# Side B's weights behind batch 2's keys, first products in pairs of blocks, and small work moved between VectorE and GpSimd

## The chip, the cores and the metric

The kernel runs on one core of a Trainium2 chip, as one program. The metric is device time in microseconds (us) of one execution; the kernel before has a median of 203.14 us over 3 runs (202.81 to 203.45). Engines are named as the profile names them: PE is TensorE's matrix products (PEld its weight loads), DVE is VectorE, ACT is ScalarE, POOL is GpSimd, and SP is SyncE, which here only issues transfers.

## The reference

Linear attention for 8 batches, then a mixture of experts with one expert per row:

```
q_s = softmax of q over the head's 64 channels
k_s = softmax of k over the 576 positions
x   = (q_s @ (k_s^T @ v)) for 8 batches x 8 heads x 576 x 64, as 4608 rows of 512
logits = x @ w_gate + modality_bias[modality_id];  e = argmax(logits)
out[row] = softmax(logits)[e] * (relu(x[row] @ w1[e]) @ w2[e])      w1: 512 x 1024, w2: 1024 x 512
```

The bias decides the expert in this draw: rows of modality 0 take one expert, those of modality 1 another. The kernel works with these two, and recomputes at the end if a row should want a third (here no row does).

## The kernel before, in words

**Places.** Each of the 4608 rows gets a place: rows of side A (one modality) fill places from the front, those of side B from the back. The running offsets (`pos`, `aoff`) are worked out on DVE in the first 12 us. From them come `slot` (which row lies in which place, L643 to L648), its digits and one-hot tables (`hhi`, `hv`, `hlo`), which PE turns into the list of rows `idx` (L718), and `bsel` (the bias of each place, L667 to L672).

**Attention, one batch at a time.** q, k and v of a batch (1152 KB each) come by SP's queue into a ring of five buffers `st` (L393). ACT takes the exponent of q in place (L821), DVE sums it (L827), and q is scaled into `eq` (L843): by DVE in batches 0 and 1, by POOL from batch 2 on. ACT takes the exponent of k into `ek` (L854); v is cast into `vb` (L864) by ACT or POOL. PE forms k^T v in two halves (L957), DVE makes `kvbd` of it (L984 to L993). PE transposes and sorts q in groups of 128 positions (L1033), ACT or DVE brings the result out of PSUM as `et` (L1045, L1047), PE multiplies by `kvbd` (L1072), and ACT or DVE copies the result into the places in `xs` (18 copies of a batch, L1103). A buffer of `st` is free for a later load once its last reader is done: the scaling for q, the exponent for k, the cast for v.

**Experts, in 9 passes of 256 places on each side.** A pass needs the batches whose rows fill its places. It has gates (L1138, L1152 to L1166), a first product of 8 blocks of 128 hidden channels, each of 4 matmuls into one PSUM bank (L1202), the relu of each block out of its bank into `hT` (L1172 on ACT, L1174 on DVE), a second product of 8 matmuls for each of two row tiles (L1215), a scaling by the gate into `y_sb` (L1178, L1180), and an indirect store by POOL (L1183). One more tile, where the two sides meet, is done near the end (L1340 to L1364).

**Weights.** `W` holds both sides' experts in bf16, cast on the way by POOL's transfers: four parts of a side (two of w1, two of w2), 8 + 4 transfers (L510, L521). Side A's first waits until k of batch 1 has landed, and q of batch 2 waits until side A's third part has landed (L403). Side B's parts have no such waits; the first two follow side A's, the others come behind `hv`.

**The order.** Each step is an `Op` with a rank and assumed costs on its engine. `Plan.order` plays the program through with these costs (which engine is idle, which ring has a free buffer) and emits the instructions in the order of that play. Each engine then takes its instructions strictly in this order, so a change of one cost or one wait can move instructions on all engines. Dead matmuls (`unread`, L1451) are put into early gaps of PE.

## Time and profile before

| | us |
|---|---|
| median of 3 runs | 203.14 |
| the profiled execution's own time | 204.96 |
| its span, first to last instruction | 203.2 |
| PE busy | 180.4 (89%) |
| DVE busy | 154.5 (76%) |
| ACT busy | 127.9 (63%) |
| POOL busy | 90.5 (45%) |

The page cuts the span into 40 slices of 5.08 us and gives the busy share of each in tenths. PE is at 9 in most slices from 30 us on; DMA is at 9 in most slices up to about 96 us, and low afterwards; loads from memory end near 117 us. The granted clock of TensorE is at half speed in one stretch near 30 us and in a shorter one near 121 us.

### The profile page before, as it was taken

The numbers are of one execution on the slowest core, as the hardware profiler recorded it, in microseconds if no ns is written. First come the engines' busy times: TensorE is split into PE (matmuls) and PEld (weight loads), VectorE is DVE, ScalarE is ACT, GpSimd is POOL, SyncE is SP. The second block draws the span as 40 slices with busy tenths as digits, with TensorE's granted clock in tenths as the row PEclk, the third lists the DMA queues.
The fourth block names the chain that finished last, engine by engine and source line by source line (L and its number), as shares of the span: only waits on it lengthen the run. The fifth ranks groups of instructions, "written<-read, shape, count | busy, mean of one in ns | idle before, by whom it ended". The sixth has DMA issues, their size and how long they took to land.

```text
span 203.2 us, 5008 instructions
## 1 busy us (share of the span) xinstructions
PE 180.4 (89%) x1716; PEld 124.4 (61%) x1735; DVE 154.5 (76%) x447; ACT 127.9 (63%) x283; POOL 90.5 (45%) x113
## 2 busy tenths in 40 slices
PE   0789679989999999999959959999999999999990
PEld 0446348577657486868647735878667657766760
DVE  1899997999879999669968973959589557755660
ACT  2669875998759599999849674999896000000100
POOL 6001910584944489943395086591303311222231
PEclk9999955999999999999999988999999999999998
DMA  6999999999999997999369711111112112121102
GB/s 191 371 400 392 186 203 225 295 394 313 280 411 404 404 399 250 390 404 338 115 201 385 271 52 55 52 53 56 53 55 103 52 55 103 52 103 56 76 28 108
DMA packets 18588, 42.33 MB, mean 208 GB/s; under 512 B 1913, under 2 KB 1913, under 8 KB 18562
## 3 DMA queue, kind: packets, MB, share of 16 engines
q1 hardware_dynamic: 13344, 28.33, 38.4%
q0 software_dynamic: 5200, 13.64, 23.3%
q8 instruction: 14, 0.23, 0.5%
q10 hardware_dynamic: 18, 0.04, 0.2%
q14 instruction: 12, 0.10, 0.1%
HBM read 36.75 MB, written 9.70 MB: 229 GB/s over the span
## 4 chain that ended last, share of the span: by engine, by line
PE 69%; DVE 11%; ACT 6%; issue 5%; POOL 3%; DMA 2%; ACTq 2%; DVEq 0%; POOLq 0%
PE ps L1215 28%; PE ps L1202 26%; DVE xs L1103 3%; PE ps L1033 3%; PE ps L1072 3%; PE ps L957 3%; ACT xs L1103 3%; PE ps L1138 2%; DVE own L827 2%; DMA bias<-n_moe_modality_bias_dram 2%; DVE eq L843 2%; POOL out_dram L1183 1%; ACT vb L864 1%; POOL eq L843 1%; ACTq L1007 1%
## 5 line engine op out<-in xcount | busy, mean ns | idle before, releaser
L1202 PE MATMUL ps<-xs,W 128*128 128x256 bf16 x576 | 71.9, 277 | 0.2
L1215 PE MATMUL ps<-W,hT 128*128 128x512 bf16 (+1 forms) x277 | 66.4, 378 | 1.1 <-issue 0.2
L1183 POOL DMA_INDIRECT out_dram<-y_sb,idx x36 | 35.7, 992 | 57.5 <-DVE y_sb L1180 30.7
L1202 PEld LDWEIGHTS <-W 128*128 128x128 bf16 x576 | 55.2, 99 | 9.8 <-issue 0.9
L1172 ACT ACTIVATE hT<-ps 128x256 bf16<-128x256 f32 x63 | 23.0, 414 | 40.7 <-PE ps L1202 40.4
L1215 PEld LDWEIGHTS <-hT 128*128 128x128 bf16 x296 | 28.6, 99 | 29.3 <-issue 1.3
L1174 DVE TENSOR_SCALAR hT<-ps 128x256 bf16<-128x256 f32 (+1 forms) x83 | 34.6, 427 | 7.4 <-PE ps L1202 4.7
L1180 DVE TENSOR_SCALAR y_sb<-ps,gate 128x512 f32<-128x512 f32 (+1 forms) x28 | 20.1, 720 | 21.1 <-PE ps L1215 15.9
L1103 ACT CAST xs<-ps 128x256 f32 (+1 forms) x99 | 31.8, 447 | 2.1 <-PE ps L957 1.0
L843 POOL TENSOR_TENSOR eq<-st,qi 128x512 bf16<-128x512 f32 (+1 forms) x30 | 28.5, 972 | 6.1 <-PE ps L1202 2.7
L827 DVE TENSOR_REDUCE own<-st 128x18 f32<-128x1152 f32 x16 | 21.6, 1350 | 0.1
L821 ACT ACTIVATE st<-st 128x1152 f32<-128x1152 f32 x16 | 18.7, 1195 | 2.8 <-DMA st<-in_q_dram 2.3
L854 ACT ACTIVATE ek<-st 128x1152 bf16<-128x1152 f32 x16 | 19.1, 1200 | 1.2 <-DMA st<-in_k_dram 1.2
L1045 ACT CAST et<-ps 128x512 bf16<-128x512 f32 (+1 forms) x30 | 16.1, 565 | 5.9 <-PE ps L1033 5.6
L1033 PE MATMUL ps<-perm,eq 128*128 128x128 bf16 x144 | 14.3, 230 | 3.5 <-POOL eq L843 2.0
L1103 DVE CAST xs<-ps 128x256 f32 (+1 forms) x45 | 16.1, 415 | 0.5 <-ACT xs L1103 0.4
L864 POOL CAST vb<-st 128x1152 bf16<-128x1152 f32 x8 | 9.0, 1142 | 16.0 <-DMA st<-in_v_dram 10.0
L1033 PEld LDWEIGHTS <-eq 128*128 128x128 bf16 x144 | 10.0, 101 | 8.2 <-POOL eq L843 3.1
L957 PE MATMUL ps<-vb,ek 64*128 64x129 bf16 x288 | 11.4, 222 | 2.7 <-ACT vb L864 2.5
L957 PEld LDWEIGHTS <-ek 64*128 64x128 bf16 x288 | 8.7, 96 | 6.7 <-issue 2.9
L1072 PE MATMUL ps<-et,kvbd 128*128 128x128 bf16 (+1 forms) x160 | 11.8, 219 | 0.2
L510 POOL DMA_DIRECT2D W<-in_moe_w_dram x8 | 5.1, 674 | 15.2 <-DMA st<-in_k_dram 15.2
(134 smaller groups left out, 170.9 us busy)
## 6 DMA issues: line engine op xcount, KB each, us to landing
st<-in_q_dram SPq DMA_DIRECT2D x6, 1152.0 KB, 12.3
st<-in_k_dram SPq DMA_DIRECT2D x6, 1152.0 KB, 13.7
st<-in_v_dram SPq DMA_DIRECT2D x6, 1152.0 KB, 12.9
st<-in_q_dram SPq DMA_DIRECT2D x4, 576.0 KB, 5.1
st<-in_k_dram SPq DMA_DIRECT2D x4, 576.0 KB, 6.7
st<-in_v_dram SPq DMA_DIRECT2D x4, 576.0 KB, 9.7
W<-in_moe_w_dram POOLq DMA_DIRECT2D x8, 256.0 KB, 6.8
W<-in_moe_w_dram POOLq DMA_DIRECT2D x4, 512.0 KB, 10.4
```

The costliest lines, as they stand in the source:

```text
L827: nc.vector.tensor_reduce(out=sums[qib.idx][:, h * NJ : (h + n) * NJ], in_=view(st[bq.idx], [[Dh, n * NJ], [1, Dh]], h * NJ * Dh), op=ALU.add,
L843: (nc.vector if e == "DVE" else nc.gpsimd).tensor_tensor(out=view(eq[eqb.idx], [[HG * Dh, n], [Dh, HG], [1, Dh]], j0 * HG * Dh), in0=view( ...
L854: nc.scalar.activation(out=view(ek[ekb.idx], [[Dh, n], [HG * Dh, NJ], [1, Dh]], h * Dh), in_=view(st[bk.idx], [[NJ * Dh, n], [Dh, NJ], [1, ...
L957: nc.tensor.matmul(out=ps_t[kvp[hg].idx][:, 130 * hp : 130 * hp + 129], lhsT=ek[ekb.idx][rows, j, P * hp : P * hp + P], rhs=vb[vbb.idx][ro ...
L1033: nc.tensor.matmul(out=view(t, [[2 * nj * 64, 2], [1, 64]], hp * nj * 64 + jj * 64), lhsT=eq[eqb.idx][:, j0 + jj, P * hp : P * hp + P], rh ...
L1103: w_ = nc.scalar.copy(out=dst, in_=src) if e == "ACT" else nc.vector.tensor_copy(out=dst, in_=src)
L1172: nc.scalar.activation(out=dst, in_=src, func=ACT.Relu)
L1174: nc.vector.tensor_scalar_max(out=dst, in0=src, scalar1=0.0)
L1180: nc.vector.tensor_scalar(out=dst, in0=src, scalar1=g, scalar2=None, op0=ALU.mult)
L1183: s_ = nc.gpsimd.indirect_dma_start(out=out, out_offset=bass.IndirectOffsetOnAxis(ap=ix[:, c : c + 1], axis=0), in_=ysb, in_offset=None, b ...
L1202: m = nc.tensor.matmul(out=t[:, 0:w], lhsT=w1(W[:, slot_, :], kd, f), rhs=xs[:, kd, lo : lo + w], start=(kd == 0), stop=(kd == KD - 1),)
L1215: nc.tensor.matmul(out=t, lhsT=h[:, kf, i * P : (i + 1) * P], rhs=W[:, slot_, W2 + kf * D + c0 : W2 + kf * D + c0 + cn], start=(kf == 0), ...
```

## The change

Side B's first part of `W` waits for k of batch 2 (POOL waits there), and q of batch 3 waits for side B's third part (SP waits there). All of batch 2's loads are planned ahead of side B's weights. `slot` and `bsel` go from DVE to POOL, and batch 2's q is scaled by DVE. The first product puts two blocks of 256 columns in one bank, and one relu takes both out. The loading of the modality ids and of the bias become two steps. Some assumed costs change, and the last passes' drains of POOL's queue.

```diff
 def dma(nbytes):
-    busy = nbytes / 390e3
+    busy = nbytes / 383e3
...
-            if src is q and b == 2:
-                behind(d, issued["w", 0, 2][-1], "the weights come first")
+            if src is q and b in (2, 3):
+                behind(d, issued["w", b - 2, 2][-1], "the weights come first")
...
-    l_ids = pl.op({"ACT": (1.2, 3.5)}, load_ids, rank=-9)
+    l_ids = pl.op({"ACT": (0.6, 3.6)}, load_ids, rank=-9)
+    l_bias = pl.op({"ACT": (0.6, 3.9)}, load_bias, rank=-8)
...
-            if not s and not part:
-                behind(issued["w", 0, 0][0], issued[k.tensor.name, 1], "the first batches come first")
+            if not part:
+                behind(issued["w", s, 0][0], issued[k.tensor.name, s + 1], "the batches ahead come first")
...
     def slot_run(_):
-        d = nc.vector
+        d = nc.gpsimd
...
     def bsel_run(_):
-        d = nc.vector
+        d = nc.gpsimd
...
-    w_in = [[load_w(0, part) for part in range(4)], []]
-    for part, nms in enumerate(("q", "k", "v", "")):
-        for nm in nms:
-            load_one(nm, 2)
-        w_in[1].append(load_w(1, part))
-    for o in w_issue[1][2:]:
-        pl.later(o, o_hv[-1])
+    w_in = [[load_w(0, part) for part in range(4)]]
+    load_batch(2)
+    w_in.append([load_w(1, part) for part in range(4)])
+    for before, o in zip([loads["k", 2][0][-1]] + w_issue[1], w_issue[1]):
+        pl.later(o, before)
...
-            if b <= 1:
+            if b <= 2:
                 ncost = on_dve(n_, 1, True)
...
+        for i in range(2):
+            for kd in range(KD):
+                f = f0 + i
+                m = nc.tensor.matmul(
+                    out=t[:, i * w : (i + 1) * w],
...
-        for f in range(KF):
+        for f in range(0, KF, 2):
...
-                    lambda e, f=f, fb=fb: relu(e, hT[hb.idx][:, f, 0:w], ps_t[fb.idx][:, 0:w]),
+                    lambda e, f=f, fb=fb: relu(
+                        e, hT[hb.idx][:, f : f + 2, 0:w], view(ps_t[fb.idx], [[w, 2], [1, w]])
+                    ),
```

What this does to the order is shown at three places. Lines of the kernel after are 1 to 9 higher than those of before.

On POOL, in the first 45 us: before, the two experts' numbers are read (`eid_i`) as soon as the constants are made, and `hv` stands between side B's first two and last two parts of `W` (64 partitions: w1; 128 partitions: w2).

```order
L353 MEMSET ex_99 128x2
L539 TENSOR_LOAD eid_i
...
L510 DMA W<-in_moe_w_dram 64x2x1024
L701 TENSOR_TENSOR hv<-hhi,vals 128x432 x6
L521 ISA
L521 DMA W<-in_moe_w_dram 128x2x1024
...
L1183 DMA out_dram<-y_sb_83,idx 4608x512
L843 TENSOR_TENSOR eq_70<-st_65,qi_86 128x512 x3
```

Now `slot` and `bsel` stand ahead of the read, and `hv` ahead of all of side B:

```order
L645 TENSOR_TENSOR slot<-na,kt 128x72
...
L670 TENSOR_TENSOR bsel<-isb,biasd 128x288
L673 TENSOR_TENSOR bsel<-bsel,bias_b 128x288
L674 TENSOR_SCALAR krow<-isb,keyd,key 128x36
L541 TENSOR_LOAD eid_i
...
L523 DMA W<-in_moe_w_dram 128x2x1024
L703 TENSOR_TENSOR hv<-hhi,vals 128x432 x6
L512 ISA
L512 DMA W<-in_moe_w_dram 64x2x1024
...
L1183 DMA out_dram<-y_sb_82,idx 4608x512
```

All four parts of side B stand behind one wait for k of batch 2, and the stores of the first pass behind them; batch 2's scaling is gone from here.

On ACT, in side A's first pass (about 31 to 36 us): before, four relus of one block each stand ahead of the first copy of batch 1 into `xs` (the copies need batch 1's last product).

```order
L1172 ACTIVATE hT_80<-ps_91 128x256
L1172 ACTIVATE hT_80<-ps_92 128x256
L1172 ACTIVATE hT_80<-ps_91 128x256
L1172 ACTIVATE hT_80<-ps_92 128x256
L1157 ACTIVATE ex_98<-L,gmx 128x8 x2
L1157 ACTIVATE ex_99<-L,gmx 128x8 x2
L1103 REGISTER_ALU
L1103 ISA
L1103 COPY xs<-ps_94 128x4x64
```

Now three relus of two blocks each stand there:

```order
L1172 ACTIVATE hT_80<-ps_92 128x2x256
L1172 ACTIVATE hT_80<-ps_91 128x2x256
L1157 ACTIVATE ex_98<-L,gmx 128x8 x2
L1172 ACTIVATE hT_80<-ps_92 128x2x256
L1157 ACTIVATE ex_99<-L,gmx 128x8 x2
L1103 REGISTER_ALU
L1103 ISA
L1103 COPY xs<-ps_94 128x4x64
```

Six blocks of the first product instead of four are ahead of batch 1's last product on PE, and so ahead of these copies.

On ACT, near the arrival of the last load, v of batch 7 (about 111 to 120 us): before, ACT casts one half of it, and relus stand behind the cast.

```order
L821 ACTIVATE st_65<-st_65 128x1152 x2
L1178 ACTIVATE y_sb_85<-ps_91,gate 128x512
L854 ACTIVATE ek_69<-st_64 128x2x9x64
L864 CAST vb_73<-st_63 128x2x9x64
L1172 ACTIVATE hT_80<-ps_95 128x256
L1172 ACTIVATE hT_80<-ps_91 128x256
L1172 ACTIVATE hT_80<-ps_93 128x256
```

Now ACT has no cast there:

```order
L821 ACTIVATE st_65<-st_65 128x1152
L1178 ACTIVATE y_sb_85<-ps_90,gate 128x512
L821 ACTIVATE st_65<-st_65 128x1152
L1172 ACTIVATE hT_80<-ps_96 128x2x256
L1172 ACTIVATE hT_80<-ps_91 128x2x256
L854 ACTIVATE ek_69<-st_67 128x2x9x64
```

POOL casts both halves instead, with batch 6's scaling behind them:

```order
L843 TENSOR_TENSOR eq_71<-st_63,qi_87 128x256
L1183 DMA out_dram<-y_sb_84,idx 4608x512
L864 CAST vb_73<-st_63 128x2x9x64
L1183 DMA out_dram<-y_sb_85,idx 4608x512
L864 CAST vb_73<-st_63 128x2x9x64
L843 TENSOR_TENSOR eq_70<-st_66,qi_86 128x512 x4
```

What waited for the last load on two engines waits for it on one.

## Rows read from the trace of the kernel before

**Rows 1.** The page's slices: PE busy, granted clock, DMA busy, in tenths.
```profile
PE   0789679989999999999959959999999999999990
PEclk9999955999999999999999988999999999999998
DMA  6999999999999997999369711111112112121102
```

**Rows 2.** Waits of PE: start, us, what [idle before <- releaser].
```profile
30.48 3.57 PE L1202 MATMUL ps<-xs,W 128*128 128x256 bf16 x16
41.85 0.35 PE L1138 MATMUL ps<-wg_sb,xs 128*128 128x8 bf16 x8 [0.85 <-ACT xs L1103]
44.45 1.33 PE L718 MATMUL ps<-hv,xs 128*128 128x72 bf16 x36
54.41 0.69 PE L957 MATMUL ps<-vb,ek 64*128 64x129 bf16 x18
57.42 3.62 PE L1215 MATMUL ps<-W,hT 128*128 128x512 bf16 x15
104.21 0.40 PE L1033 MATMUL ps<-perm,eq 128*128 128x128 bf16 x4 [2.03 <-POOL eq L843]
118.90 0.61 PE L1138 MATMUL ps<-wg_sb,xs 128*128 128x8 bf16 x16 [2.03 <-ACT hT L1172]
```

**Rows 3.** Stretches: length, busy time (instructions) of each engine, PEclk, DMA share, GB/s.
```profile
10.00:20.00 10.00, 9.22 (x97) 5.31 (x96) 9.88 (x33) 8.08 (x10) 0.60 (x1) 1.00 1.05 397
20.00:25.00 5.00, 3.10 (x44) 1.80 (x42) 4.78 (x14) 4.59 (x8) 5.00 (x9) 0.96 1.09 200
30.40:34.80 4.40, 4.40 (x34) 3.40 (x31) 3.36 (x17) 2.12 (x8) 0.00 (x0) 0.50 1.12 217
120.40:123.20 2.80, 2.77 (x8) 0.84 (x9) 0.87 (x1) 1.11 (x2) 2.53 (x3) 0.50 0.24 92
```

**Rows 4.** SP's issues of loads, and the landing times of L393's transfers.
```profile
30.84 0.37 SPq L393 DMA_DIRECT2D st<-in_q_dram  x1
109.07 0.37 SPq L393 DMA_DIRECT2D st<-in_v_dram  x1
DMA to landing us min/median/max: 4.2/10.7/23.3
```

**Rows 5.** POOL in order of time.
```profile
19.40 2.65 POOL L510 DMA_DIRECT2D W<-in_moe_w_dram  x4 [15.16 <-DMA st<-in_k_dram]
65.02 2.24 POOL L864 CAST vb<-st 128x1152 bf16<-128x1152 f32 x2 [1.94 <-DMA st<-in_v_dram]
99.69 2.23 POOL L864 CAST vb<-st 128x1152 bf16<-128x1152 f32 x2 [6.02 <-PE ps L957]
105.38 3.67 POOL L843 TENSOR_TENSOR eq<-st,qi 128x512 bf16<-128x512 f32 x4
118.84 0.98 POOL L1183 DMA_INDIRECT out_dram<-y_sb,idx  x1 [0.16 <-ACT hT L1172]
```

**Rows 6.** ACT in order of time.
```profile
42.39 1.30 ACT L821 ACTIVATE st<-st 128x1152 f32<-128x1152 f32 x1
117.41 1.16 ACT L864 CAST vb<-st 128x1152 bf16<-128x1152 f32 x1 [2.45 <-DMA st<-in_v_dram]
```

**Rows 7.** Groups by form: line, engine, operation, count | busy us, mean ns | idle before.
```profile
L843 POOL TENSOR_TENSOR eq<-st,qi 128x512 bf16<-128x512 f32 x24 | 24.9, 1060 | 6.1 <-PE ps L1202 2.7 <-DVE qi L839 2.4 <-ACT ex L1157 0.7
L1174 DVE TENSOR_SCALAR hT<-ps 128x256 bf16<-128x256 f32 x81 | 33.2, 421 | 6.7 <-PE ps L1202 4.7 <-PE ps L1138 0.6 <-ACT hT L1172 0.2
L1172 ACT ACTIVATE hT<-ps 128x256 bf16<-128x256 f32 x63 | 23.0, 414 | 40.7 <-PE ps L1202 40.4
L1045 ACT CAST et<-ps 128x512 bf16<-128x512 f32 x24 | 14.2, 604 | 5.2 <-PE ps L1033 4.9
L843 DVE TENSOR_TENSOR eq<-st,qi 128x512 bf16<-128x512 f32 x8 | 5.2, 684 | 0.0
L1174 DVE TENSOR_SCALAR hT<-ps 128x512 bf16<-128x512 f32 x2 | 1.4, 692 | 0.7 <-PE ps L1351 0.5
```

More of the change, by code (lines that the diff above doesn't have):

```diff
@@ L435, in load_ids, with load_bias @@
         )
+    def load_bias(_):
         nc.scalar.dma_start(
@@ L495, in experts @@
         d.tensor_sub(out=keyd, in0=key[:, 1:2], in1=key[:, 0:1])
-    o_parts = pl.op({"DVE": (0.35, 0.5)}, parts_run, [l_ids, c_dve], rank=-5)
+    o_parts = pl.op({"DVE": (0.35, 0.5)}, parts_run, [l_bias, c_dve], rank=-5)
     o_spread = pl.op({"PE": (0.2, 0.45)}, spread_run, [o_parts, c_pool], rank=-5, takes=[b_buf])
@@ L756 @@
     o_off = pl.op({"DVE": (1.0, 1.2)}, off_run, [o_pos], rank=-5, uses=[r_buf])
-    o_vals = pl.op({"DVE": (0.7, 0.85, True)}, vals_run, [c_dve2], rank=15)
-    o_slot = pl.op({"DVE": (1.17, 1.3, True)}, slot_run, [o_off], rank=15)
-    o_digits = pl.op({"DVE": (0.5, 0.65, True)}, digits_run, [o_slot], rank=15)
+    o_vals = pl.op({"DVE": (0.7, 0.85)}, vals_run, [c_dve2], rank=-4)
+    o_slot = pl.op({"POOL": (1.3, 1.45, True)}, slot_run, [o_off], rank=12)
+    o_digits = pl.op({"DVE": (0.5, 0.65, True)}, digits_run, [o_slot], rank=12)
     o_hhi = [pl.op(on_dve(HC * NSL // 3), hhi_run(i), [o_digits], rank=15) for i in range(3)]
@@ L767 @@
     o_idx = pl.op({"DVE": (0.4, 0.6)}, idx_run, [o_id], rank=16, uses=[id_buf])
[L768 removed]
+    o_bsel = pl.op({"POOL": (1.8, 2.0, True)}, bsel_run, [o_off, o_exp], rank=13)
     o_mid = pl.op({"DVE": (1.0, 1.15, True)}, mid_run, [o_idx, o_bsel], rank=74)
[L771 to L777 removed]
+    w_in = [[load_w(0, part) for part in range(4)]]
[3 more added lines that the diff above has]
+        pl.later(o, before)
     for b in range(3, B):
@@ L1198, in w1, with h_mm @@
         return view(t, [[2, P]], kd * F + f // 2 * 2 * P + f % 2)
-    def h_mm(t, lo, w, slot_, f, whole=False):
-        for kd in range(KD):
-            m = nc.tensor.matmul(
-                out=t[:, 0:w],
-                lhsT=w1(W[:, slot_, :], kd, f),
-                rhs=xs[:, kd, lo : lo + w],
-                start=(kd == 0),
-                stop=(kd == KD - 1),
-            )
-            if whole and not f and not kd:
-                for w_ in final[-2:]:
-                    sync(m, w_, "every batch is in its places")
+    def h_mm(t, lo, w, slot_, f0, whole=False):
+        for i in range(2):
[3 more added lines that the diff above has]
+                    out=t[:, i * w : (i + 1) * w],
+                    lhsT=w1(W[:, slot_, :], kd, f),
+                    rhs=xs[:, kd, lo : lo + w],
+                    start=(kd == 0),
+                    stop=(kd == KD - 1),
+                )
+                if whole and not f and not kd:
+                    for w_ in final[-2:]:
+                        sync(m, w_, "every batch is in its places")
     def y_mm(t, h, i, slot_, c0=0, cn=D):
@@ L1243, in ffn @@
         )
-        g3 = pl.op({"DVE": (0.18, 0.36)}, lambda _: gates3(t0, nt, ex[xb.idx]), [g2], rank=rank_g, uses=[xb])
+        g3 = pl.op({"DVE": (0.32, 0.45)}, lambda _: gates3(t0, nt, ex[xb.idx]), [g2], rank=rank_g, uses=[xb])
         hs = []
-        for f in range(KF):
+        for f in range(0, KF, 2):
             fb = Buf(r_ps)
             hm = pl.op(
-                on_pe(*[w] * KD),
+                on_pe(*[w] * (2 * KD)),
                 lambda _, f=f, fb=fb: h_mm(ps_t[fb.idx], lo, w, side, f, whole),
@@ L1302, in ffn @@
         if n >= 5 and not last:
-            pl.op({"POOL": (3.0, 3.0)}, lambda _: nc.gpsimd.drain(), [st_], rank=-1)
+            drain = lambda _: nc.gpsimd.drain()
+            if (n, lo, w) == passes_a[-1]:
+                pl.op({"POOL": (2.0, 2.0)}, drain, evs, rank=-0.5)
+            else:
+                pl.op({"POOL": (3.0, 3.0)}, drain, [st_], rank=-1)
         return g3
@@ L1424, in ffn_rest @@
         ym = pl.op(
-            on_pe(*[D] * KF), y_rest(fb), [*hs, *wc], rank=500 + rank + 0.2, takes=[fb], uses=[hb, wb[1]]
+            on_pe(*[D] * KF), y_rest(fb), [*hs, *wc], rank=500 + rank + 0.4, takes=[fb], uses=[hb, wb[1]]
         )
```

5 lines of the change are left out of this document (2 added, 3 removed).

## The prediction

> **What bounds the kernel now.** I read the page's slices first: PE is busy in nearly all of them from the seventh on, and DMA in nearly all up to the nineteenth [rows 1]. So two things run side by side until about 96 us, and after 124 us PE runs alone. With PE full over most of the span, a change helps only where it takes away PE's idle time, its half-clock time, or the start-up ahead of the first expert product at 30.48 us [rows 2]. I therefore went through PE's waits in order of time, and for each to the engine named and that engine's own wait.
>
> Between 30.5 us and 124 us there are four places of size. (a) The granted clock is 0.50 from 30.4 to 34.8 [rows 3]: 4.4 us at 1.2 instead of 2.4 GHz, 2.2 us lost. (b) At 41.85 PE has waited 0.85 us for ACT's copies of batch 1 into `xs` [rows 2]. (c) At 104.21 it has waited 2.03 us for POOL's scaling of batch 5 [rows 2], which stands on POOL behind the casts of batch 6's v at 99.69 [rows 5]; I read that start as the landing of that v, since the PE work named there had long been done. (d) At 118.90 it has waited 2.03 us for ACT's relus [rows 2], because ACT stood 2.45 us for the last load, v of batch 7, before its cast at 117.41 [rows 6]; then the clock is 0.50 from 120.4 to 123.2 [rows 3], another 1.4 us. The rest are waits of half a microsecond and less, mostly behind DVE's copies of batch 2 into `xs`, 1.5 us together by my estimate.
>
> **The change part by part.** *The weights' waits.* q of batch 2 is issued at 30.84 as before, since it waits for the same third part of side A [rows 4]. Now nothing of side B travels with it. 1.18 MB at 397 GB/s [rows 3] are 3.0 us. The shortest landing is 4.2 us [rows 4], of a transfer of half that size, which leaves 2.7 us of set-up. So q2 lands at 36.5, k2 at 39.5, v2 at 42.4. POOL began side A's weights at 19.40 [rows 5] and the third part had landed at 30.84: 11.4 us for three parts, and 2.6 us for each further one (0.52 MB written at 200 GB/s [rows 3]). Side B's parts then land at about 45.7, 48.3, 50.9 and 53.5, and q of batch 3 at 56.6. PE comes to side B's first product only after side A's second pass and batch 2's sorting, at about 54, so some 5 us cover the new wait. Behind the waiting POOL stand only side B's own transfers and the first stores (`hv` is ahead of it); behind the waiting SP the rest of batch 3. Both set-ups lie beside a transfer in flight (v2, then side B's fourth part), so I cost them at 0; uncovered they are 2.7 us each. The gain is at most one part, 2.6 us; I take the stream of loads as 1 us earlier, since batch 3's v lands near 62.5 and was cast at 65.02 as it landed [rows 5], and part of that is given back to the stores.
>
> The Trainium skill, "DMA: Bandwidth & Descriptors" (Rules for kernel authors), says to issue a transfer early and wait late, so that the fixed set-up overlaps; this change issues two groups later. That bears on the mechanism of the first rival.
>
> *`slot` and `bsel` on POOL, batch 2's scaling on DVE.* Eight forms of small instructions go ahead of side A's weights on POOL. The nearest row is the 512-element scaling at 1060 ns [rows 7]; as an upper end that is 8.5 us from 12 us on, so 20.5 against the 19.40 at which POOL stops waiting for k of batch 1; a lower end is 2 us. I take 3, hidden by that wait: 0, and at most 1.1 us later weights. DVE gives these up and takes four scalings of 684 ns and a half one, 3.1 us: even. POOL is freed of 4.9 us near 50 us, where it was not the bound.
>
> *Blocks in pairs.* A pair costs DVE 692 ns instead of 2 x 421, ACT about 604 (a 512-column copy, the nearest row) instead of 2 x 414 [rows 7]. With 40 and 32 pairs that is 6.0 us of DVE and 7.2 us of ACT. Neither is the bound, so I credit only 0.6 us, out of the 1.5 us of small waits.
>
> *What the order makes of it.* On PE six blocks of A's first product instead of four come ahead of batch 1's last product. At 3.57 us for 16 matmuls [rows 2], at the low clock, the 8 more delay it by 1.8 us, and with it ACT's copies and, behind them, the exponent of q2 (42.39 before [rows 6]), to 44.2 or later. So the earlier landing of batch 2 is not used. Wait (b) would grow to 2.7, but the 1.33 us of `idx` products [rows 2] now stand ahead of it: net +0.5 to +1.4, I take 0.9. Then k^T v of batch 2, which ran at 54.41 [rows 2], is wanted at about 50, while ACT has its operands only at about 51: +1.0. By the second product of B's first pass (57.42 before [rows 2]) PE is 2 us behind on the same work.
>
> *The last loads.* v7 is issued at 109.07, when POOL has ended the scaling of batch 5 (105.38 + 3.67) [rows 4, 5], and that chain starts with v6's landing at 99.7. With the stream 1 us earlier, batch 5's scaling begins 1 us earlier and one store fewer stands ahead of it (0.98 [rows 5]), just when PE comes: wait (c) goes, -2.0. v7 lands at 116.4. ACT no longer stands at its cast, so (d) in its old form goes: -2.0 and -1.4. PE alone is then at +0.9 +1.0 -0.6 -2.0 -2.0 -1.4 = -4.1 us.
>
> What is late next is POOL: two casts (2.23), one store (0.98) and the first scaling of batch 6 (1.06) [rows 5, 7] end 4.3 us after v7, at 120.7. Before, PE passed that point at 123.8 (gates and a block from 118.90, eight second products that end at 123.2, batch 7's first k^T v of 0.7 [rows 2, 3]). So the end moves by -3.1, not by -4.1: PE waits 1.0 there, too little to expect a fall of the clock, as after (c). The other scalings of batch 6 follow at 1.06 us each between PE's other work: +0.4.
>
> Sum: -4.1 + 1.0 + 0.4 = -2.7 us. (a) and the start-up stay as they are: the scaling of batch 1 on DVE, which paces PE up to 30 us, is not touched, and the steps before it change places at equal length. The profiled execution took 204.96 us for its span of 203.2; so 202.3 by its count, and against the median of 203.14, 200.4 us.
>
> **Rivals.** *First, slower: the two waits open the loads' queue.* If a set-up of 2.7 us lies bare at k2 and again before q3, the stream is up to 5.4 us late where it is full, and v7 with it. From v7 on all is fixed: the scaling of batch 6 is there at v7 + 4.3, and 0.4 is lost behind it. So the change is slower once v7 lands after 119.1, 1.7 us later than before. With v7 3.1 us late: 203.14 + 1.4 = 204.5. For it: DMA's slices have been full with no wait there [rows 1]. Against it: other transfers are in flight at both moments.
>
> *Second: the stream gains more.* If the freed time of POOL, DVE and ACT lets buffers come free 3 us earlier, v7 lands before 115, POOL's chain ends before PE needs it, and what is left is PE alone, -4.1, with some of the +1.9 at the start hidden: 198.4. For it: 13 us of relu time saved. Against it: relus are not what frees a buffer.
>
> *Third: the clock.* The new fillers around batch 1's k^T v could keep TensorE at 2.4 GHz through A's first product: -2.2, and the 1.8 us of delay halves. Alone this ends at POOL's chain and changes nothing; with the second rival it gives 196.5. The opposite, a fall after the longer wait at 42 us, costs 1.4 and is hidden in the same way unless v7 is early.
>
> *Fourth: no difference.* The +1.9 at the start stays, and (c) and (d) only change their names, within 0.6 us of 203.14.
>
> **How the numbers follow.** The forecast 200.4, with its own range 199.2 to 202.4, gets 0.40; the second and third rival 0.25; no difference 0.14; the first rival and others on its side 0.21. Less than 0.3% (0.6 us) can't be told from no change here. So faster 0.40 + 0.25 = 0.65, same 0.14, slower 0.21. The range goes from 197.2, between the two better cases, to 204.5, the first rival's time.
>
> **What would show it.** Right: ACT has no wait for v near 117, PE's last long wait names POOL's `eq`, the wait near 42 us for ACT's copies is above 1.3 us, and v7 lands between 115 and 117. The step on the weights is wrong if PE's first product of side B waits for a transfer, or if DMA shows an empty stretch between 30 and 60 us. The step on the start is wrong if the granted clock is 1.00 at 32 us, or if A's first product begins more than 1 us away from 30.5. The whole is wrong if v7 lands after 119.

## The result, and the profile after

The changed kernel takes 204.83 us (median of 4 runs, 204.48 to 205.54) against 202.97 us (4 runs, 201.88 to 203.45) for the kernel before: a ratio of 1.0104 with a 95% interval of 1.0054 to 1.0153. It is 1% slower; 200.4 was forecast. Measured again (a_again below) it came to 204.72 against 203.16, which is 0.8% by the medians; the recorded ratio is 1.0157 (1.0089 to 1.0224). Throughout, medians are over all runs of a kernel and ratios, as they were recorded, over its undisturbed ones, so that in kernels with a wide spread the two can point different ways. For a_again and b_slot the recorded ratio is higher than the listed times give (0.8% and 2.4% by the medians), and I go by the medians there.

The profiled execution took 204.96 us with a span of 203.4, and that is the usual case for the changed kernel. The one that was profiled of the kernel before also took 204.96 us, and there it was 2.0 above the median. Both profiled executions therefore took the same time although the kernels differ; the first experiment below deals with this.

The page's slices after (PE busy, granted clock, DMA busy, GB/s), to lay beside [rows 1]:

```profile
PE   1987769989899899799999999999899999999980
PEclk9999975999999999999999999999999999999999
DMA  5999999959999999999749810111202112121112
GB/s 190 368 401 391 177 193 280 400 157 149 210 387 397 396 401 405 392 398 375 291 148 370 329 64 31 72 68 40 88 22 103 52 55 103 52 85 73 52 52 110
```

PE no longer shows the two 5s near 104 and 119 us, nor the low clock behind the second. DMA has a 5 in the ninth slice (40.7 to 45.8 us). In the two behind it DMA looks full, but moves 149 and 210 GB/s, where slices full of loads move about 400; the slices of side A's weights, the fifth and sixth, move 177 and 193.

PE's waits (start, us, what, [idle before <- releaser]), answering [rows 2]:

```profile
30.30 5.11 PE L1205 MATMUL ps<-xs,W 128*128 128x256 bf16 x24
40.58 1.33 PE L720 MATMUL ps<-hv,xs 128*128 128x72 bf16 x36
42.77 0.35 PE L1138 MATMUL ps<-wg_sb,xs 128*128 128x8 bf16 x8 [0.85 <-ACT xs L1103]
48.91 0.68 PE L957 MATMUL ps<-vb,ek 64*128 64x129 bf16 x18
53.88 3.65 PE L1205 MATMUL ps<-xs,W 128*128 128x256 bf16 x32 [0.73 <-DVE y_sb L1180]
82.49 0.69 PE L957 MATMUL ps<-vb,ek 64*128 64x129 bf16 x18 [1.48 <-POOL vb L864]
118.71 0.55 PE L1138 MATMUL ps<-wg_sb,xs 128*128 128x8 bf16 x16
121.99 0.40 PE L1033 MATMUL ps<-perm,eq 128*128 128x128 bf16 x4 [0.37 <-POOL eq L843]
146.04 0.96 PE L1138 MATMUL ps<-wg_sb,xs 128*128 128x8 bf16 x32 [0.83 <-DVE hT L1174]
```

The waits of 2.03 us near 104 and 119 are gone, as forecast; the gates at 118.71 wait for nothing. The wait near 42 us has not grown. New are 0.73 us at 53.88, 1.48 at 82.49 for a cast of batch 4's v, and 0.83 at 146.04.

POOL, SP and ACT in order of time, answering [rows 4, 5, 6]:

```profile
8.11 0.34 POOL L645 TENSOR_TENSOR slot<-na,kt 128x72 f32<-128x72 f32 x1 [3.56 <-DVE na L613]
13.29 0.36 POOL L674 TENSOR_SCALAR krow<-isb,keyd,key 128x36 f32<-128x36 f32 x1
19.89 2.69 POOL L512 DMA_DIRECT2D W<-in_moe_w_dram  x4 [6.24 <-DMA st<-in_k_dram]
33.56 3.51 POOL L703 TENSOR_TENSOR hv<-hhi,vals 128x432 bf16<-128x432 bf16 x4 [0.55 <-DVE hhi L691]
43.10 0.66 POOL L512 DMA_DIRECT2D W<-in_moe_w_dram  x1 [6.04 <-DMA st<-in_k_dram]
81.30 2.23 POOL L864 CAST vb<-st 128x1152 bf16<-128x1152 f32 x2 [1.93 <-DMA st<-in_v_dram]
```

```profile
55.03 0.37 SPq L393 DMA_DIRECT2D st<-in_q_dram  x1
110.36 0.37 SPq L393 DMA_DIRECT2D st<-in_v_dram  x1
```

```profile
63.84 1.17 ACT L821 ACTIVATE st<-st 128x1152 f32<-128x1152 f32 x1 [3.73 <-DMA st<-in_q_dram]
```

`slot` and `bsel` are done at 13.65. `hv` ends at 37.1, where it began at 38.07 before. POOL then stands 6.04 us for k of batch 2, and side B's weights are issued from 43.10. q of batch 3 is issued at 55.03 (32.40 before). ACT stands 3.73 us for that q. The POOL cast at 81.30 waits for batch 4's v, and PE at 82.49 waits for the cast: the late stream of loads reaches PE through this chain.

Stretches (columns as in [rows 3]): first the two in which the clock was 0.50 before, then single microseconds around the start of side B's weights.

```profile
30.40:34.80 4.40, 4.40 (x24) 3.09 (x21) 3.40 (x13) 1.56 (x5) 3.01 (x4) 0.50 1.03 256
120.40:123.20 2.80, 2.43 (x30) 1.34 (x29) 2.24 (x7) 1.46 (x4) 2.80 (x4) 1.00 0.23 86
41.00:42.00 1.00, 0.91 (x29) 0.79 (x25) 1.00 (x2) 1.00 (x5) 0.00 (x0) 1.00 0.94 348
42.00:43.00 1.00, 0.23 (x9) 0.24 (x10) 0.97 (x3) 1.00 (x4) 0.00 (x0) 1.00 0.23 88
43.00:44.00 1.00, 1.00 (x19) 0.91 (x17) 0.24 (x2) 1.00 (x2) 0.66 (x1) 1.00 0.06 25
48.00:49.00 1.00, 0.89 (x8) 0.21 (x8) 1.00 (x3) 1.00 (x2) 0.71 (x1) 1.00 0.88 117
```

Most packets of batch 2's loads are through at 42 us, but POOL's wait for the middle one, k, ends only at 43.1. In between the queues carry 25 to 88 GB/s. By the packets in the trace (their first starts at 44.5), side B's parts then land at 48.7, 51.7, 54.1 and 57.2, and q of batch 3 at 62.1 (53.7 before).

The relus of the pairs (count | busy us, mean ns | idle before), answering [rows 7]:

```profile
L1174 DVE TENSOR_SCALAR hT<-ps 128x512 bf16<-128x512 f32 x42 | 28.9, 688 | 10.6 <-PE ps L1205 6.3 <-PE ps L1072 2.6 <-PE ps L1360 0.4
L1172 ACT ACTIVATE hT<-ps 128x512 bf16<-128x512 f32 x32 | 19.3, 627 | 7.7 <-PE ps L1205 7.7
```

A pair costs 688 and 627 ns, where 692 and 604 were assumed.

### The profile page after: what moved, and what is told of

It is laid out like the page before. It is cut to its first block, busy times and chain, and to the rows that moved or that the text cites. A ratio compares the mean times of both kernels' runs of the same rounds, so it can differ in the third digit from the quotient of the medians.

```text
span 203.4 us, 4937 instructions
## 1 busy us (share of the span) xinstructions
PE 180.4 (89%) x1736; PEld 123.0 (60%) x1736; DVE 149.5 (74%) x398; ACT 124.4 (61%) x254; POOL 92.4 (45%) x119
## 4 chain that ended last, share of the span: by engine, by line
PE 41%; DMA 19%; POOL 12%; ACT 10%; issue 7%; DVE 7%; SPq 1%; ACTq 1%; POOLq 0%; DVEq 0%
PE ps L1205 19%; PE ps L1218 17%; DMA st<-in_v_dram 16%; POOL eq L843 7%; POOL out_dram L1183 4%; ACT xs L1103 4%; DMA st<-in_k_dram 3%; ACT ek L854 2%; ACT hT L1172 1%; PE ps L1033 1%; DVE own L827 1%; POOL vb L864 1%; SPq L393 1%; ACT vb L864 1%; DVE hT L1174 1%
## 5 line engine op out<-in xcount | busy, mean ns | idle before, releaser
L1205 PE MATMUL ps<-xs,W 128*128 128x256 bf16 x576 | 70.9, 278 | 1.1 <-DVE y_sb L1180 0.7
L1205 PEld LDWEIGHTS <-W 128*128 128x128 bf16 x576 | 56.1, 100 | 10.9 <-issue 1.5
L1174 DVE TENSOR_SCALAR hT<-ps 128x512 bf16<-128x512 f32 x42 | 28.9, 688 | 10.6 <-PE ps L1205 6.3
L1180 DVE TENSOR_SCALAR y_sb<-ps,gate 128x512 f32<-128x512 f32 (+1 forms) x26 | 18.9, 725 | 19.6 <-PE ps L1218 16.5
L843 POOL TENSOR_TENSOR eq<-st,qi 128x512 bf16<-128x512 f32 (+1 forms) x25 | 23.7, 972 | 2.1 <-DVE qi L839 1.9
L1172 ACT ACTIVATE hT<-ps 128x512 bf16<-128x512 f32 x32 | 19.3, 627 | 7.7 <-PE ps L1205 7.7
L1033 PE MATMUL ps<-perm,eq 128*128 128x128 bf16 x144 | 13.4, 224 | 3.7 <-DVE eq L843 1.7
L864 POOL CAST vb<-st 128x1152 bf16<-128x1152 f32 x10 | 11.2, 1145 | 10.8 <-DMA st<-in_v_dram 10.4
L957 PE MATMUL ps<-vb,ek 64*128 64x129 bf16 x288 | 11.0, 217 | 3.9 <-POOL vb L864 1.5
L1033 PEld LDWEIGHTS <-eq 128*128 128x128 bf16 x144 | 9.1, 99 | 8.2 <-DVE eq L843 3.7
L957 PEld LDWEIGHTS <-ek 64*128 64x128 bf16 x288 | 8.3, 93 | 8.6 <-issue 4.0
L1072 PEld LDWEIGHTS <-kvbd 128*128 128x128 bf16 x160 | 9.6, 98 | 2.0 <-DVE kvbd L993 0.7
```

The costliest lines, as they stand in the source:

```text
L843: (nc.vector if e == "DVE" else nc.gpsimd).tensor_tensor(out=view(eq[eqb.idx], [[HG * Dh, n], [Dh, HG], [1, Dh]], j0 * HG * Dh), in0=view( ...
L957: nc.tensor.matmul(out=ps_t[kvp[hg].idx][:, 130 * hp : 130 * hp + 129], lhsT=ek[ekb.idx][rows, j, P * hp : P * hp + P], rhs=vb[vbb.idx][ro ...
L1033: nc.tensor.matmul(out=view(t, [[2 * nj * 64, 2], [1, 64]], hp * nj * 64 + jj * 64), lhsT=eq[eqb.idx][:, j0 + jj, P * hp : P * hp + P], rh ...
L1072: nc.tensor.matmul(out=view(ps_t[xbuf.idx], [[1, nj * 64]], c * nj * 64), lhsT=kvbd[kvb.idx][:, c, :], rhs=et[etb.idx][:, c, j0 * 64 : (j0 ...
L1172: nc.scalar.activation(out=dst, in_=src, func=ACT.Relu)
L1174: nc.vector.tensor_scalar_max(out=dst, in0=src, scalar1=0.0)
```

## The experiments

The groups of runs were measured on different chips, each beside the kernel before; what compares is the difference from the time in the fourth column. Part 1 is the two waits with the new order of the loads, part 2 is GpSimd's share (`slot`, `bsel` and their ranks).

| run | what it is | median us | before beside it | ratio (95%) |
|---|---|---|---|---|
| b_again | before, unchanged | 203.43 | 203.46 | 1.0005 (0.9957 to 1.0052) |
| a_nowait | after, neither wait | 203.09 | 203.46 | 0.9897 (0.9835 to 0.9958) |
| a_noq3 | after, q's wait away | 207.21 | 203.40 | 1.0198 (1.0141 to 1.0255) |
| a_nowb | after, weights' wait away | 206.22 | 203.40 | 1.0091 (1.0018 to 1.0164) |
| b_loads | before + part 1 | 206.73 | 203.46 | 1.0143 (1.0100 to 1.0187) |
| a_oldloads | after - part 1 | 209.03 | 203.40 | 1.0294 (1.0234 to 1.0354) |
| b_slot | before + GpSimd's share | 207.99 | 203.16 | 1.0300 (1.0226 to 1.0374) |
| a_mix | a_oldloads + one wait | 203.68 | 203.16 | 1.0003 (0.9954 to 1.0052) |
| a_v7act | a_nowait + last casts on ACT | 204.00 | 203.16 | 0.9946 (0.9894 to 0.9999) |
| a_again | after, unchanged | 204.72 | 203.16 | 1.0157 (1.0089 to 1.0224) |
| a_wq2 | after, first wait earlier | 204.68 | 203.87 | 1.0059 (1.0017 to 1.0101) |
| a_q3w1 | after, second wait earlier | 206.85 | 203.87 | 1.0092 (1.0039 to 1.0145) |
| a_wq2q3w1 | after, both earlier | 204.29 | 203.87 | 0.9969 (0.9909 to 1.0029) |
| a_nopair | after - pairs | 205.76 | 203.46 | 1.0122 (1.0078 to 1.0166) |
| b_pairs | before + pairs | 202.33 | 203.40 | 0.9981 (0.9932 to 1.0029) |
| b_pairs2 | the same again | 202.64 | 202.84 | 1.0031 (0.9998 to 1.0063) |
| b_nq2 | before + batch 2 on DVE | 205.11 | 203.87 | 1.0035 (0.9980 to 1.0089) |
| b_rest | before + pairs, costs, ranks | 204.04 | 202.84 | 1.0076 (1.0036 to 1.0117) |

**Was the profile the usual one?** b_again has no edit.

> The kernel before, unchanged, for a second profile and for the granted clock of its timed runs. The profiled execution that the prediction was read from took 204.96 us, 2.0 above the median of 202.97. Theory A (the waits that were to go are not in the usual execution): a median near 203.0 with a span near 201.4, and between 98 and 126 us of the profile PE loses clearly less than the 7.1 us of the first profile (waits of 2.03 at 104.21 and 118.90, half clock from 120.4). Theory B (the change itself adds more than it takes, the profile was typical): the same waits of about 2 us near 104 and 119 again. The mean clock tells: above 0.975 for A, near 0.964 for B.

Two waits and two stretches of its profile (span 201.0, mean clock 0.981):

```profile
103.80 0.40 PE L1033 MATMUL ps<-perm,eq 128*128 128x128 bf16 x4 [1.74 <-POOL eq L843]
118.40 0.61 PE L1138 MATMUL ps<-wg_sb,xs 128*128 128x8 bf16 x16 [1.96 <-ACT hT L1172]
```

```profile
30.40:34.80 4.40, 4.34 (x51) 3.60 (x51) 3.98 (x21) 2.70 (x9) 0.00 (x0) 0.70 1.12 210
120.40:123.20 2.80, 2.80 (x30) 1.38 (x28) 1.06 (x5) 2.06 (x6) 2.63 (x4) 1.00 0.09 28
```

Neither theory holds whole. The two long waits belong to the kernel. The half clock behind the second does not: after nearly the same wait the clock stays at 1.00. In the early stretch it is 0.70 and not 0.50. By the rows that is 1.4 us and 0.2 x 4.4 = 0.9 us, together 2.3, and the spans differ by 2.2. Between these two executions the difference is thus about what the clock explains. It is no rule for the others: of b_again's runs the one with 205.46 us had a mean clock of 0.979, the one with 202.43 us 0.971.

PE's busy time in three stretches then gives a first account of where the changed kernel loses (first the kernel before in this second profile, then the changed one):

```profile
66.00:98.50 32.50, 32.00 (x356) 22.52 (x354) 27.51 (x73) 30.01 (x79) 20.29 (x21) 1.00 0.97 360
98.50:126.00 27.50, 23.66 (x288) 16.78 (x287) 21.94 (x64) 19.41 (x36) 18.38 (x19) 1.00 0.51 178
126.00:150.00 24.00, 23.94 (x244) 17.32 (x242) 17.71 (x69) 22.98 (x65) 9.32 (x10) 1.00 0.15 57
```

```profile
66.00:98.50 32.50, 29.55 (x318) 20.47 (x316) 21.81 (x53) 28.01 (x70) 24.01 (x24) 1.00 1.04 394
98.50:126.00 27.50, 27.08 (x323) 18.73 (x322) 23.72 (x64) 23.25 (x39) 18.16 (x18) 1.00 0.54 195
126.00:150.00 24.00, 22.27 (x235) 16.62 (x233) 15.10 (x53) 20.11 (x55) 10.53 (x12) 1.00 0.18 68
```

The clock is 1.00 in all six. The change loses 2.45 us from 66 to 98.5, wins 3.42 to 126 and loses 1.67 to 150. With 0.35 lost from 35.4 to 66 by the same view and about 1.0 of clock from 30.4 to 35.4 (0.53 against 0.73 over 5 us) that is 2.05 of the 2.4 us between the spans. One pair of executions is a rough measure: in a_again's profile the same three figures are 30.01, 26.68 and 22.88. Nor is a busy stretch a gain by itself, since work that comes late in one stretch fills the next.

**The two waits.** Three kernels leave the order on every engine as it is and only take waits away (`k` and `q` in the lines are batch 2's and 3's).

```diff
 a_nowait: both edits;  a_noq3: the first;  a_nowb: the second
-            if src is q and b in (2, 3):
+            if src is q and b == 2:
-            if not part:
+            if not s and not part:
                 behind(issued["w", s, 0][0], issued[k.tensor.name, s + 1], ...)
```

> The changed kernel without its two new waits (side B's first weights no longer wait for k of batch 2, q of batch 3 no longer for side B's third part); the order on every engine is the same. Theory C (the first rival: the two waits open the queue of loads, q of batch 3 lands at 62.1 instead of 53.7 and PE waits between 66 and 98 us for batches 3 to 5): q of batch 3 lands before 58, v of batch 4 before 76 instead of 78.9, PE's loss between 66 and 98 us falls from 3.9 to under 1.5, and the median falls by 1.5 to 3 us to 202 to 203.3. Theory D (the waits are covered; the loss is the order's or the pairs'): the median stays within 0.6 of 204.8.

> The changed kernel without the wait of q of batch 3 for side B's third part; the wait of side B's first weights for k of batch 2 stays, and so does every order. If q's wait is the dear one (it keeps SP's queue empty from 45.2 to 58.0 us): q of batch 3 lands before 55 instead of 62.1, v of batch 5 before 87, and the median comes down to 202.5 to 203.8, as without both (203.09). If the weights' wait is the dear one: 204.2 to 205, and PE waits at side B's second product, since the weights share the queue with batch 3 and land after 59.

> The changed kernel without the wait of side B's first weights for k of batch 2; q of batch 3 still waits for side B's third part. The weights are then issued at 37.1 us, when POOL has ended hv, and not at 43.1: the third part lands near 50 instead of 54.1, q of batch 3 near 57.5 instead of 62.1. If the lost time is how late batch 3 comes, whichever wait does it: 203.3 to 204.3, between the changed kernel and the one without both. If only q's wait counts: 204.2 to 205.

Without both, q of batch 3 lands at 51.7, PE is busy 31.92 us from 66 to 98.5, and the median goes from 1.6 to 1.9 us above the kernel before to 0.4 below it: theory C. With one wait alone the median is 3.8 us (a_noq3) and 2.8 us (a_nowb) above the kernel before. That is worse than with none; that it is worse than with both is not shown for a_nowb, whose ratio of 1.0091 is no higher than the changed kernel's. Neither kernel came out in the times expected of it. With the weights' wait alone, q of batch 3 lands at 46.0, before the weights begin, and k and v of batch 3 run beside them; their last part lands at 64.2, and PE waits for them (in an execution of 211.46 us; the others took 205.70 to 209.09):

```profile
56.56 3.44 PE L1205 MATMUL ps<-xs,W 128*128 128x256 bf16 x30 [1.75 <-DMA W<-in_moe_w_dram]
64.72 4.17 PE L1218 MATMUL ps<-W,hT 128*128 128x512 bf16 x12 [1.98 <-DMA W<-in_moe_w_dram]
```

With q's wait alone the third part landed at 49.3 and q at 57.7, as expected, but ACT waited 1.76 us for batch 2's v and the time did not follow. So q's wait keeps the loads off the weights, and the weights' wait keeps the weights off batch 2's v. In a_nowait ACT stands 1.85 us for that v. Its runs go from 199.88 to 205.52, those of the kernel before beside it from 202.46 to 205.11; that the wider spread comes from having neither wait is not shown.

**Part 1 in the old order, and the change without it.** a_oldloads undoes all of part 1; b_loads puts it alone into the kernel before.

```diff
-    w_in = [[load_w(0, part) for part in range(4)], []]   # b_loads; a_oldloads the other way round
-    for part, nms in enumerate(("q", "k", "v", "")):
-        ...
-    for o in w_issue[1][2:]:
-        pl.later(o, o_hv[-1])
+    w_in = [[load_w(0, part) for part in range(4)]]
+    load_batch(2)
+    w_in.append([load_w(1, part) for part in range(4)])
+    ...
```

> The kernel before with the first part of the change alone: the two waits, batch 2's loads planned ahead of all of side B's weights, and these behind hv. Theory C: q of batch 3 lands near 61 as in the changed kernel and the median rises to 204 to 205.5. Theory D: within 0.6 of 203.0.

> The changed kernel with the whole first part undone: no new waits, side B's parts planned between batch 2's q, k and v, and two of them ahead of hv; pairs, GpSimd's share, VectorE's scaling and the costs stay. Theory C (part 1 costs about 2 to 3 us, the rest of the change gains about 1): 201.0 to 202.8, below the kernel before. Theory D' (in the new order the rest loses as well): 203.0 to 204.5. Between 98 and 126 us the wait for the scaling on POOL should be under 1 us in C.

Part 1 alone costs 3.3 us (q of batch 3 at 62.6, v of batch 7 at 120.5). That bears out theory C, with more than I had put on it. Its largest wait of PE before 100 us is 2.60 us at 67.27 for ACT, which had itself stood 3.25 us for q of batch 3; right behind it the clock is 0.60 and 0.54 from 68 to 72. But the changed kernel without part 1 is 5.6 us above the kernel before, against both expectations. Its PE, ACT and POOL:

```profile
54.07 1.89 PE L1220 MATMUL ps<-W,hT 128*128 128x512 bf16 x4 [5.64 <-ACT hT L1174]
```

```profile
52.37 1.16 ACT L856 ACTIVATE ek<-st 128x1152 bf16<-128x1152 f32 x1 [4.60 <-DMA st<-in_k_dram]
```

```profile
33.70 3.51 POOL L703 TENSOR_TENSOR hv<-hhi,vals 128x432 bf16<-128x432 bf16 x4 [0.55 <-DVE hhi L691]
37.15 1.48 POOL L523 DMA_DIRECT2D W<-in_moe_w_dram  x2
```

In the kernel before the same two parts were issued six microseconds later, behind a later `hv`:

```profile
38.07 5.24 POOL L701 TENSOR_TENSOR hv<-hhi,vals 128x432 bf16<-128x432 bf16 x6 [12.13 <-DVE hhi L689]
43.27 1.48 POOL L521 DMA_DIRECT2D W<-in_moe_w_dram  x2
```

`slot` on GpSimd, with its new rank, brings `hv` forward, and with it side B's last two parts, onto the loads of batch 2. (Before, `slot` ran on DVE at 35.2; whether the engine or the rank makes it early was not tried apart.) Two runs test that: GpSimd's share alone, and one wait put back.

```diff
 b_slot (before; bsel_run, costs and ranks likewise):
     def slot_run(_):
-        d = nc.vector
+        d = nc.gpsimd
 a_mix (a_oldloads):
+            if s and part == 2:
+                behind(issued["w", s, 2][0], issued[k.tensor.name, 2], ...)
+    pl.later(w_issue[1][2], loads["k", 2][0][-1])
```

> The kernel before with slot and bsel on GpSimd alone (and the ranks that go with it). Theory F: this brings hv forward by 5 to 7 us (it began at 38.07), and with it the two parts of side B's weights that are queued behind hv; they then share the DMA queues with k and v of batch 2, ScalarE stands for k of batch 2 and PE waits for it near 54 us, as in the changed kernel with the old order of loads (k of batch 2 at 49.6 instead of 43.8, PE's wait 5.64 us): 206 to 209.5. My prediction's step (hidden before 19.4, cost 0): within 0.6 of 203.4.

> The changed kernel with the old order of loads, in which only side B's third part waits for k of batch 2, and q of batch 3 for nothing. Theory F: what cost 5.64 us in the old order of loads was the third and fourth part beside k of batch 2; with them behind it the time falls from 209.0 by 4 to 6 us, to 203 to 205. Theory G (in this order of the program something else is slow, for example ScalarE's place of the cast of batch 2's v): over 206.

By the medians b_slot is 4.8 us slower than the kernel before, and a_mix stands 0.5 us above it where a_oldloads stood 5.6. b_slot's profiled execution is its fastest (203.89; the others go from 207.11 to 211.89), and even there the two parts are issued at 38.55 and ACT waits 0.81 us for k and 2.18 for v of batch 2. What the slower ones did, no trace shows, so the size of 4.8 us rests on the median alone. Theory F's mechanism is seen at both ends: GpSimd's share with its ranks, which I had costed at 0, is dear unless something holds the weights back. So part 1's first wait is needed by part 2, and must not be judged without it.

**Which effect of the waits is dear.** Three kernels with the changed order, and waits for one transfer earlier.

```diff
 a_wq2: first edit;  a_q3w1: second;  a_wq2q3w1: both
-                behind(issued["w", s, 0][0], issued[k.tensor.name, s + 1], ...)
+                behind(issued["w", s, 0][0], issued[(q if s else k).tensor.name, s + 1], ...)
-                behind(d, issued["w", b - 2, 2][-1], ...)
+                behind(d, issued["w", b - 2, 4 - b][-1], ...)
```

> The changed kernel, its order untouched, with side B's first weights waiting for q of batch 2 instead of k. Theory H (the stream is lost in the stretch from 42 to 44.5 us, in which the queues stand nearly empty because POOL learns of k's landing at 43.1 and its first packets come 1.4 us later): third part near 51 instead of 54, q of batch 3 near 58.5 instead of 62, median 203.0 to 204.2 against about 204.8. Theory I (the weights now run beside v of batch 2 and ScalarE stands for its cast, as without any wait): ScalarE waits 2 us or more for v near 48, and 204.5 to 206.5.

> The changed kernel, its order untouched, with q of batch 3 waiting for side B's second part instead of the third. Theory J (the set-up of q of batch 3, 3.0 us from its issue at 55.03 to its first packet at 58.0, and the four stores beside it are what makes the stream late): q of batch 3 lands near 59.5, v of batch 5 at 86.5 to 87.5 instead of 88.5, and the median falls by 0.8 to 2 us. Rival: the last two parts of the weights now share the queues and land after 59.5, PE waits for them at side B's second product, and the median stays or rises.

> The changed kernel, its order untouched, with both waits one transfer earlier: side B's weights behind q of batch 2, q of batch 3 behind side B's second part. If H and J both hold, 201.8 to 203.3, below the kernel before (203.3); if either wait protects something (I, or the rival of J), 204 or more.

a_wq2 fills the stretch from 42 us (third part at 50.5, q at 58.5, as H had it), and at the same time ACT pays I's price:

```profile
48.62 1.15 ACT L864 CAST vb<-st 128x1152 bf16<-128x1152 f32 x1 [2.43 <-DMA st<-in_v_dram]
```

Its median of 204.68 is outside H's range and in I's; its ratio lies under the changed kernel's two, with overlapping intervals. a_q3w1 brings q to 59.8 and gains nothing; its median is 3.0 us above the kernel before, and J is not borne out alone. With both, the stream is early (v of batch 7 at 114.6). PE in the trace of a_wq2 (first two lines), of a_q3w1 (third) and of a_wq2q3w1:

```profile
35.40:66.00 30.60, 26.92 (x260) 18.32 (x261) 25.68 (x64) 22.36 (x46) 10.44 (x13) 0.94 1.05 315
66.00:98.50 32.50, 31.66 (x360) 23.57 (x364) 25.48 (x58) 29.28 (x70) 23.14 (x23) 1.00 1.03 389
66.00:98.50 32.50, 29.71 (x322) 20.90 (x326) 22.27 (x52) 27.80 (x69) 22.26 (x22) 1.00 1.03 386
66.00:98.50 32.50, 31.66 (x345) 22.77 (x347) 25.14 (x58) 29.29 (x71) 22.97 (x23) 1.00 0.97 367
98.50:126.00 27.50, 25.32 (x305) 17.92 (x305) 22.86 (x66) 21.61 (x42) 19.25 (x20) 1.00 0.50 178
126.00:150.00 24.00, 22.62 (x226) 16.53 (x227) 15.09 (x58) 20.56 (x56) 8.75 (x9) 1.00 0.15 57
```

The stretch from 66 us comes back as soon as side B's weights start earlier, also in a_wq2 alone (31.66) and in a_nowb (31.92), and it does not with q alone (29.71). The order on every engine is the same in these kernels, so that the time between the same two instructions can be compared. From the first k^T v (L957) of batch 3 to the first of batch 4 it is 11.03 us in both profiles of the changed kernel (71.46 to 82.49, 70.90 to 81.93) and 11.08 in a_q3w1 (69.30 to 80.38), but 8.99 to 9.00 in a_wq2, a_wq2q3w1, a_nowb and a_nowait (for example 72.16 to 81.15 in a_wq2). So 2.0 us are what the weights' wait costs there, through batch 4's v.

What starting the weights earlier costs lies ahead of that: in a_wq2 PE waits 2.26 us at 49.83 for the cast of batch 2's v, and behind it the clock is 0.64 from 50 to 54. In a_wq2q3w1 ACT waits 1.05 us for that v, and the clock stays at 1.00. The earlier q can't be the reason, since q of batch 3 is issued only at 49.91, after that cast; whether moving q as well is worth anything is therefore open. The time of a_wq2q3w1 is level with the kernel before, ratio 0.9969. Its median of 204.29 is outside the 201.8 to 203.3 expected, its profiled execution (202.54) is inside; what made the others slower is not shown.

**The chain behind v of batch 7.**

```diff
 a_v7act (a_nowait):
-        if b < 2:
+        if b < 2 or b == B - 1:
             vcost = on_act(S * 2)
```

> The changed kernel without its two new waits, and with the casts of batch 7's v on ScalarE alone. Without the waits PE still stood 1.97 us at 120.61 for the first scaling of batch 6, which is queued on POOL behind two casts of v of batch 7 and a store, as the prediction had it (v7 + 4.3 us). If that chain is the cause: the wait goes and the median is 201 to 202.5. If ScalarE is late instead (its casts of 1.16 hold up the relus, as in the kernel before at 118.90): 203 to 204.

Not settled. PE's wait of 1.97 us for POOL's first scaling is gone from its trace, but 1.97 us at 122.53, put down to VectorE's `L`, stand in its place, in an execution of 208.20 us in which ACT waited 5.24 us for batch 2's v, and PE 5.07 for its cast; the runs go from 200.77 to 208.20.

> The changed kernel unchanged, on the same chip as the others of this call: 204.5 to 205.5 and 0.7 to 1.3% above the kernel before, if the first comparison stands, and 2 us or more above the version without its two waits and with the last casts on ScalarE, if the waits are what costs it. Its profile should again show third weights part at 54, q of batch 3 at 62, and a wait of about 1.5 us for a cast of v near 82.

The second measurement of the changed kernel agrees with the first: parts at 53.1 (third) and q of batch 3 at 61.0, again 1.48 us for the cast of v, at 81.93.

**Pairs, VectorE's scaling, and the rest.** b_rest is b_pairs with ids and bias in two steps, the planner's new costs and ranks (but not those of `slot`, `bsel` and what hangs on them), and the drain.

```diff
 a_nopair (after), b_pairs (before, the other way round):
-        for f in range(0, KF, 2):
+        for f in range(KF):
         ...                              # h_mm and the relu likewise
 b_nq2 (before):
-            if b <= 1:
+            if b <= 2:
```

> The changed kernel with its first products in single blocks per bank again, each with its own relu of 128x256. Theory C: the pairs are not the cause; the credit of 0.6 that I gave them is lost, 204.8 to 205.6. Rival theory E (a pair holds PE and the bank longer, so that the first second product waits for a relu of 0.69 instead of 0.42 us, nine times a side): 203.0 to 204.2.

> The kernel before with the pairs alone. Undoing the pairs in the changed kernel took it from about 204.8 to 205.8, so they are worth 0.9 us there; my credit was 0.6. If that holds in the old order: 202.3 to 203.0 against 203.4. If it was the new order that needed them: 203.0 to 204.0.

> The kernel before with the pairs alone, once more, as the version that may beat both kernels: 0.5% below the kernel before (first time 202.33 against 203.40, ratio 0.998 with an interval of 0.993 to 1.003). If that was chance: within 0.3% of it.

> The kernel before with batch 2's q scaled by VectorE alone. My prediction had this as even on VectorE and no bound on POOL: within 0.6 of 203.3. Rival: it frees POOL of 4.9 us near 50 us and moves the stores forward, 202.0 to 202.7; or VectorE, busy for 9.3 of 10 us there, delays the copies into xs, 203.9 to 205.

> The kernel before with the pairs and the small rest of the change (ids and bias in two steps, the planner's costs and ranks, the drain), without the loads' waits, GpSimd's share and VectorE's scaling. If the loss is that of the three parts left out, this stays at or below the kernel before: ratio 0.990 to 1.001. If the new costs and ranks alone make a slower order (batch 1's last product later by 1.8 us, as in the prediction's step on the start): 1.003 to 1.010.

The pairs alone make no difference that two measurements can tell. Theory E is not borne out: without them the changed kernel is not faster. In b_pairs2 PE has no wait above 0.3 us between 43 and 140, and yet little is won, in part since the wait for ACT's copies into `xs` has grown from 0.83:

```profile
42.54 0.35 PE L1138 MATMUL ps<-wg_sb,xs 128*128 128x8 bf16 x8 [2.02 <-ACT xs L1103]
```

That is the prediction's step on the start (six blocks ahead of batch 1's last product), seen without the `idx` products in front. b_nq2 leaves its cost between -0.2% and +0.9%. b_rest is slower by 0.8%: the new costs and ranks are not neutral for the order either. The end of the program stays open: from 126 to 150 us PE is busy 23.94 us before, 22.27 after, and in the changed kernel without pairs

```profile
126.00:150.00 24.00, 23.54 (x256) 17.84 (x254) 16.39 (x55) 21.46 (x63) 12.52 (x13) 1.00 0.18 68
```

This points to the pairs, whose relus PE waits for at 146.04, but that kernel's order differs too. Against the pairs as the only cause, b_pairs and b_pairs2 are busy 23.58 and 23.41 there, and a_again 22.88 with its wait (0.69 at 144.35) for ACT's copies. No version beats both kernels by more than its interval, except a_nowait and, barely, a_v7act by their ratios; by the medians they are 0.4 us below and 0.8 above the kernel before, and the spread of their runs forbids more.

## Why the prediction was wrong

- **The waits (c) and (d) go: right, the size in part by luck.** ACT has no wait for v at 117, and PE's last longer waits there name POOL's `eq`. PE gains 3.42 us from 98.5 to 126 by the second profile, where the working had -2.0, -2.0 and +1.4 for POOL's chain, -2.6 net. But some of the 3.42 is work that had come late from 66 on: in a_nowait and a_wq2q3w1, where it does not, the stretch holds 25.26 and 25.32, a gain of 1.6 to 1.7. And POOL's chain, forecast to hold PE 1.0, holds it 0.37 at 121.99, where PE comes late; in a_nowait, where PE is there 3 us earlier, it is 1.97 at 120.61.
- **The clock behind (d): counted twice.** The profiled execution lay 1.8 us above the median of 203.14. I took this off as a constant (202.3 became 200.4) and also credited 1.4 us for the low clock at 120.4. The second profile has no low clock there: the same 1.4 us was in both. Without it the forecast is 201.8.
- **Side B's weights and q of batch 3, cost 0: wrong, and this decides.** The step hid both set-ups beside other transfers: k at 39.5, the first part at 45.7, one every 2.6 us behind it, q at 56.6. POOL learned of k at 43.10 and the four parts took from 44.5 to 57.2, 3.2 us each. q was issued at 55.03, its first packet came 3.0 us later, and it landed at 62.1. "5 us cover the new wait" was true of the weights (PE had side B's first product at 53.88 without waiting for them). It was not asked who else stood behind: batches 3 to 5, which cost PE 2.45 us from 66 to 98.5 (1.99 in a_again's profile). 2.0 us lie between batch 3's k^T v and batch 4's, and go in each of the four kernels whose weights start earlier. The prediction's own sign against this step, an empty stretch of DMA between 30 and 60 us, is there from 42 to 44.
- **The first rival had the mechanism, not the place.** It decided by v of batch 7 after 119.1. That landed at 117.0, 0.2 later than before; the loss fell 20 to 50 us earlier. From 66 to 98.5 PE waits 0.52 us at 68.71 for a relu of ACT, which had stood for q of batch 3, 1.48 at 82.49 for the cast of batch 4's v, 0.38 at 90.17 for POOL's scaling and 0.32 at 92.01 for a relu of DVE. Part 1 alone, b_loads, is that rival in full, v of batch 7 at 120.5 and 3.3 us slower, where the rival's time was 1.4 us above the median. The Trainium skill's rule cited there (issue early, wait late; "DMA: Bandwidth & Descriptors", Rules for kernel authors) has the trace on its side, 25 to 88 GB/s between 42 and 44 us; but a_noq3 and a_wq2 show that an earlier issue costs as well what it runs beside: PE's 1.98 us for the weights at 64.72, and 2.26 for batch 2's v at 49.83.
- **`slot` and `bsel`: the size was right, the step was incomplete.** They end at 13.65, well ahead of 19.89. I left out what their being early moves: `hv`, and the DMAs queued behind it on POOL, 4.8 us in b_slot by its median. Part 1's first wait holds these DMAs back, so this step does not show in the changed kernel.
- **Start: +1.9 forecast (+1.3 with the pairs' 0.6), about 1.35 seen, otherwise made up: luck.** The wait at 42.77 is 0.85, not above 1.3: the `idx` products cover it. The +1.0 for k^T v of batch 2 is not seen, for it runs at 48.91 without a wait. From 35.4 to 66 PE loses 0.35, and the clock from 30.4 to 35.4 another 1.0, which differs between two executions of the kernel before as well (0.56 and 0.73).
- **Pairs, 0.6 credited: not seen.** Two runs in the old order say zero, and 1.67 us from 126 to 150 (1.06 in a_again's profile), perhaps partly theirs, was not in the sum.
- **The third rival's 196.5** does not follow from its own terms: 198.4 - 2.2 is 196.2, and less if the delay halves. The bottom of the range hangs on it, the result does not, since the clock was again 0.50 from 30.4 to 34.8.
